# Gated linear attention with an MLP on one core: transposes of seven pairs by transfers within SBUF, DMA issues on two queues, a new order

## The chip, the cores and the metric

The kernel runs on one core of a Trainium2 chip. The metric is the device time of one execution in microseconds. Engines are named as in the profile: PE (TensorE, products), PEld (its weight loads), DVE (VectorE), ACT (ScalarE), POOL (GpSimd) and SP (SyncE, which here only issues transfers). A name with a q, as ACTq, is the engine's queue issuing a transfer.

## What is computed

Two parts in a row. The first is a recurrent linear attention with a decay for each key channel, over 4 batches, 8 heads, 768 steps and 48 channels:

```python
for t in range(S):
    state = alpha[:, :, t, :, None] * state + einsum('bhd,bhe->bhde', k[:, :, t], v[:, :, t])
    y[:, :, t] = einsum('bhd,bhde->bhe', q[:, :, t], state)
```

Its result, with the heads side by side, is a matrix x of 3072 x 384. The second part is an MLP with a cosine gate:

```python
h = x @ w_in            # 384 x 2048
g = h * cos(h)
out = g @ w_out         # 2048 x 384
```

## The kernel before

The sequence of one batch is cut into three pieces of 256 steps, so there are 12 pieces, called pairs (J = 0 to 11; J // 3 is the batch). A pair lies with two neighbouring steps on each of 128 partitions (e = 0, 1), and is worked as two chunks of 64 partitions (c = 0, 1).

The steps of one pair, by the names in the plan:

- `load a|k|q|v` (L108 to L119): one transfer of 384 KB each from SP's queue into rings of buffers (four for a, three for the others). `load a 3` waits for the last product of `yT 1`, so that later inputs stay behind the weights; everything behind it on SP's queue waits too. `w1`, `w2` (L131, L134): the weights, from POOL's queue.
- `mula`, `ln`, `cums0`, `cums`, `sub`, `icp`, `exps`, `eb`: the logarithm of the decay, its running sums by a triangular product on PE, and their exponentials on ACT (`eb` is four exponentials and the next pair's `ln` together). ACT loads a table whenever it changes between these and the cosine (L143, L388).
- `sk`, `sq` (L228, L232): k times the inverse decay into `kh`, q times the decay into `qh`, for e = 0 and 1, on DVE (":D" in the plan) or POOL. `kh` and `qh` are bf16 tiles of [128, e, head, 64], 48 channels padded to 64, three of each.
- `castv` (L235): v to bf16. `vst` (L241): four transfers of 64 KB within SBUF that stack the values of the two steps under each other in `vs` (two buffers), for pairs 3 to 11; for pairs 0 to 2, `vpe` and `vev` do it by products and evictions.
- `trans` (L274): 32 products on PE that transpose 64 x 128 pieces of `kh` and `qh` into PSUM. `evT` (L287): two copies of it into `qkT` in SBUF (three buffers), one for each chunk, on DVE or ACT (":A").
- `scores` (L295), `mask` (L300): 8 products for each chunk into `A_ps`, and the causal mask on DVE into `A_sb`.
- `outer`, `add`, `state` (L312, L326 or L328, L334), `decay`: the state at the chunk's end.
- `yT` (L361), `evy` (L372): the output y, transposed, from state and scores, and its eviction into `xT` on ACT or DVE.
- `m1` (L382), `sin` (L388), `gate` (L393), four of each: 12 products into `h_ps`, the cosine on ACT, the gate on DVE.
- `m2` (L411; L405 for the last), four quarters of four products for each half of the rows, `evo` (L423, L419) and `out` (L429): the output, its eviction into one of four buffers and its store of 192 KB on SP's queue; the last one goes in two halves, on ACT's and SP's queues.
- `idle` (L437): products of zeros that fill PE's time at the start.

The order is written out by hand: a table `PLAN` gives each step of each pair a place, all steps are sorted by place, and `tc.manual_schedule()` issues each engine's instructions in that order. Each engine and each queue works in order; waits between them come from the data. So a place says what stands ahead of a step on its own queue, not when it starts. An entry "2850:A" is place 2850 on ACT.

`h_ps`, `A_ps`, `T_ps` and some others share three turns of a PSUM tile of two banks (tag "h").

## Time and profile before

| | |
|---|---|
| median of 3 runs | 183.17 us (183.09 to 183.19) |
| profiled execution, its own time | 182.95 us |
| span of its profile | 181.1 us |
| mean granted TensorE clock | 0.999 |
| instructions | 5764 |
| read from HBM, written | 25.17 MB, 4.72 MB |
| tables loaded by ACT | 16, 1283 ns each |
| idle products on PE | 11.1 us busy |

The profile is of one execution. Its page gives the busy time of each engine, the chain of work that ended last (followed back from the last instruction, at each step to what released it), groups of instructions by source line with mean duration and the idle time before them, and the transfers by issue. The span goes from the first to the last instruction; the execution's own time has 1.85 us around it. In rows of the timeline, the columns are start, length, engine, line, operation, tiles; in brackets stands the idle time before and what ended it.

### The profile page before, as it was taken

The numbers are of one execution on the slowest core, as the hardware profiler recorded it, in microseconds if no ns is written. First come the engines' busy times: TensorE is split into PE (matmuls) and PEld (weight loads), VectorE is DVE, ScalarE is ACT, GpSimd is POOL, SyncE is SP. The second block draws the span as 40 slices with busy tenths as digits, with TensorE's granted clock in tenths as the row PEclk, the third lists the DMA queues.
The fourth block names the chain that finished last, engine by engine and source line by source line (L and its number), as shares of the span: only waits on it lengthen the run. The fifth ranks groups of instructions, "written<-read, shape, count | busy, mean of one in ns | idle before, by whom it ended". The sixth has DMA issues, their size and how long they took to land.

```text
span 181.1 us, 5764 instructions
## 1 busy us (share of the span) xinstructions
PE 174.6 (96%) x2467; PEld 133.1 (73%) x2470; DVE 132.6 (73%) x181; ACT 128.5 (71%) x169; POOL 72.6 (40%) x104
## 2 busy tenths in 40 slices
PE   7999899988999999999999999999999999999993
PEld 2445689756697876876799759678787878879672
DVE  7189677668899898796869965896987886653700
ACT  3847677997888999898598995997457428544520
POOL 5046730369682625805895196297003010000000
PEclk9999999999999999999999999999999999999999
DMA  6999999999969978984939953662202400102022
GB/s 149 261 270 227 204 211 224 272 254 268 274 160 270 282 183 233 295 249 106 264 73 290 251 149 101 161 164 78 71 0 49 145 5 0 47 0 79 11 87 87
DMA packets 57801, 29.47 MB, mean 163 GB/s; under 512 B 50992, under 2 KB 56496, under 8 KB 57776
## 3 DMA queue, kind: packets, MB, share of 16 engines
q1 hardware_dynamic: 56256, 25.86, 57.3%
q0 software_dynamic: 1376, 3.15, 9.4%
q8 instruction: 19, 0.31, 0.7%
q10 hardware_dynamic: 144, 0.10, 0.2%
q14 instruction: 6, 0.05, 0.1%
HBM read 25.17 MB, written 4.72 MB: 165 GB/s over the span
## 4 chain that ended last, share of the span: by engine, by line
PE 89%; DMA 3%; ACT 2%; DVE 2%; POOL 1%; issue 1%; POOLq 0%
PE h_ps L382 34%; PE o_ps L411 30%; PE idle_ps L437 6%; PE y_ps L361 5%; PE A_ps L295 3%; DMA k<-in_k_dram 3%; PE T_ps L274 3%; PE U_ps L312 3%; PE o_last L405 1%; PE cums_h L162 1%; DVE gsb L393 1%; ACT c_sb L388 1%; PE cums L162 1%; POOL kh L228 1%; PE vs_ps L250 1%; ACT xT L372 1%
## 5 line engine op out<-in xcount | busy, mean ns | idle before, releaser
L393 DVE TENSOR_TENSOR gsb<-h_ps,c_sb 128x1024 bf16<-128x1024 f32 x48 | 57.9, 1221 | 22.2 <-ACT c_sb L388 21.6
L388 ACT ACTIVATE c_sb<-h_ps,halfpi 128x1024 bf16<-128x1024 f32 x48 | 53.2, 1115 | 27.0 <-PE h_ps L382 24.3
L382 PE MATMUL h_ps<-xT,w 128*128 128x256 bf16 x576 | 67.5, 273 | 0.3 <-DVE gsb L393 0.2
L411 PE MATMUL o_ps<-w,gsb 128*128 128x384 bf16 x368 | 66.2, 326 | 0.6 <-DVE o_sb L423 0.6
L382 PEld LDWEIGHTS <-w 128*128 128x128 bf16 x576 | 62.2, 114 | 3.2 <-issue 0.4
L411 PEld LDWEIGHTS <-gsb 128*128 128x128 bf16 x368 | 34.5, 98 | 21.3 <-issue 0.9
L334 POOL TENSOR_TENSOR un<-us,c 128x384 bf16<-128x384 f32 x20 | 16.9, 845 | 38.6 <-DVE us L326 35.9
L300 DVE TENSOR_TENSOR A_sb<-A_ps,msk 128x1024 bf16<-128x1024 f32 x24 | 28.8, 1215 | 2.6 <-PE A_ps L295 2.6
L232 POOL TENSOR_TENSOR qh<-q,cp 128x384 bf16<-128x384 f32 x13 | 13.4, 1031 | 14.7 <-ACT cp L216 12.4
L228 POOL TENSOR_TENSOR kh<-k,icp 128x384 bf16<-128x384 f32 x15 | 15.7, 1052 | 5.6 <-DMA k<-in_k_dram 5.4
L156 POOL TENSOR_TENSOR a<-a 128x384 f32<-128x384 f32 x9 | 9.0, 1002 | 13.1 <-DMA a<-in_alpha_dram 13.1
L437 PE MATMUL idle_ps<-zeros 128*128 128x512 bf16 x38 | 11.1, 438 | 1.4 <-DVE halfpi L77 1.2
L148 ACT ACTIVATE lna<-a 128x768 bf16<-128x768 f32 x12 | 10.1, 842 | 3.0 <-DMA a<-in_alpha_dram 3.0
L235 POOL CAST vp<-v 128x768 bf16<-128x768 f32 x12 | 10.5, 880 | 2.5 <-DMA v<-in_v_dram 2.5
L423 ACT COPY o_sb<-o_ps 128x384 f32<-128x384 f32 x13 | 6.1, 481 | 7.5 <-PE o_ps L411 7.4
L372 ACT CAST xT<-y_ps 128x384 bf16<-128x384 f32 x16 | 8.8, 599 | 2.9 <-PE y_ps L361 2.6
L143 ACT ACT_TABLE_LOAD x8 | 10.3, 1283 | 0.9 <-PEq L552 0.7
L287 ACT COPY qkT<-T_ps 128x1024 bf16<-128x1024 bf16 x10 | 9.8, 1016 | 1.0 <-PE T_ps L274 1.0
L388 ACT ACT_TABLE_LOAD x8 | 10.3, 1283 | 0.1
L287 DVE COPY qkT<-T_ps 128x1024 bf16<-128x1024 bf16 x14 | 9.2, 684 | 1.4 <-PE T_ps L274 1.4
L232 DVE TENSOR_TENSOR qh<-q,cp 128x384 bf16<-128x384 f32 x11 | 6.8, 627 | 4.5 <-ACT cp L216 2.9
L326 DVE TENSOR_TENSOR us<-U_ps,un 128x384 f32<-128x384 f32 x16 | 8.8, 550 | 1.4 <-PE U_ps L312 1.3
(70 smaller groups left out, 157.2 us busy)
## 6 DMA issues: line engine op xcount, KB each, us to landing
a<-in_alpha_dram SPq DMA_DIRECT2D x12, 384.0 KB, 6.1
q<-in_q_dram SPq DMA_DIRECT2D x12, 384.0 KB, 5.8
k<-in_k_dram SPq DMA_DIRECT2D x12, 384.0 KB, 5.7
v<-in_v_dram SPq DMA_DIRECT2D x12, 384.0 KB, 5.7
out_dram<-o_sb SPq DMA_DIRECT2D x23, 192.0 KB, 2.5
vs<-vp SPq DMA_DIRECT2D x36, 64.0 KB, 2.6
w<-in_moe_w_in_dram POOLq DMA_DIRECT2D x2, 768.0 KB, 9.4
w<-in_moe_w_out_dram POOLq DMA_DIRECT2D x4, 384.0 KB, 9.0
```

Of the source, the lines that this page charges most:

```text
L228: eng.tensor_tensor(out=kh_t[J % NQ][:, e, :, 0:D], in0=kqv["k", J][:, :, e], in1=icp_, op=ALU.mult)
L232: eng.tensor_tensor(out=qh_t[J % NQ][:, e, :, 0:D], in0=kqv["q", J][:, :, e], in1=cp, op=ALU.mult)
L235: nc.gpsimd.tensor_copy(out=vp_t[J % NV][:, :, :, 0:D].rearrange("s e h d -> s h e d"), in_=kqv.pop(("v", J)))
L287: apart(("T", J), copy(out=qkT_sb[J][:, c], in_=T_ps[J][:, c].rearrange("r n e s -> r n (e s)")))
L300: nc.vector.tensor_tensor(out=A_sb[J][:, c].rearrange("s a p t -> s (a p) t"), in0=A_ps.pop((J, c)).rearrange("s a p t -> s (a p) t"), in1 ...
L334: nc.gpsimd.tensor_tensor(out=u, in0=U_sum.pop(n), in1=c2_sb[J][:, :, c].unsqueeze(3).to_broadcast([C, NP, 2, D]), op=ALU.mult)
L372: apart(("y", J), copy(out=xT[J][:, :, c * C : (c + 1) * C].rearrange("r i (t e) -> r i e t", e=2), in_=y_ps[J][c][:, 0 : KT * C].rearrang ...
L382: nc.tensor.matmul(h_ps[J, u][:, f, :], cols, xT[J][:, kk, :], start=(kk == 0), stop=(kk == KT - 1))
L388: nc.scalar.activation(out=c_sb[J, u], in_=h_ps[J, u], func=AF.Sin, bias=halfpi, scale=1.0)
L393: nc.vector.tensor_tensor(out=gsb[J][:, u * FW : (u + 1) * FW], in0=h_ps.pop((J, u)), in1=c_sb.pop((J, u)), op=ALU.mult)
L411: nc.tensor.matmul(o_ps[J, c][:, 0:DM], gsb[J][:, ft, c * C : (c + 1) * C], w2[:, ft], start=(ft == 0), stop=(ft == NF - 1))
L437: nc.tensor.matmul(idle_ps[0], zeros[:, 0:C], zeros, start=True, stop=True)
```

## The change

`kh` and `qh` are laid out anew, [128, p, e, a, 64], where p is the pair of heads and a the head in it, so that 128 values of one p and e lie side by side. The products of `sk` and `sq`, `trans` and `outer` address the new layout; their sizes stay.

For pairs 5 to 11 `trans` and `evT` go. In their place stand `trd 1` (k) and `trd 0` (q): each issues two transfers from SP's queue, one for each chunk, that read 64 partitions of 1024 bf16 values in SBUF and write them transposed into `qkT`.

15 of the 24 stores, and the stacked copies (`vst`) of pairs 4 and 9, are issued from ACT's queue. `load` can name a queue too, and stays on SP. ACT's table of exponentials is asked for at the start of the schedule.

The table of places is new throughout. Some steps change engine: `sk` on DVE 9 to 4, `sq` on DVE 11 to 4 (the rest on POOL), `evy` on ACT 16 to 11, `evT` on ACT 10 to 3 and on DVE 14 to 7. The number of idle products goes from 41 to 40.

```diff
-            t = consts.tile([C, 2, H, 64], BF, tag=f"{nm}{r}", name=f"{nm}{r}")
+            shape = [C, NP, 2, 2, 64] if nm in ("kh", "qh") else [C, 2, H, 64]
+            t = consts.tile(shape, BF, tag=f"{nm}{r}", name=f"{nm}{r}")
...
     def scale_k(J, e, eng):
-        icp_ = icp_sb.pop((J, e)).rearrange("p (h d) -> p h d", h=H)
-        eng.tensor_tensor(out=kh_t[J % NQ][:, e, :, 0:D], in0=kqv["k", J][:, :, e], in1=icp_, op=ALU.mult)
+        icp_ = icp_sb.pop((J, e)).rearrange("s (p a d) -> s p a d", p=NP, a=2)
+        eng.tensor_tensor(out=kh_t[J % NQ][:, :, e, :, 0:D], in0=kqv["k", J][:, :, e].rearrange("s (p a) d -> s p a d", a=2),
+                          in1=icp_, op=ALU.mult)
...
-    def stack_v(J):
+    def stack_v(J, queue):
...
-                nc.sync.dma_start(out=vs[HC * e : HC * e + HC, c].rearrange("s h d -> s (h d)"),
-                                  in_=vp[HC * c : HC * c + HC, e].rearrange("s h d -> s (h d)"))
+                queue.dma_start(out=vs[HC * e : HC * e + HC, c].rearrange("s h d -> s (h d)"),
+                                in_=vp[HC * c : HC * c + HC, e].rearrange("s h d -> s (h d)"))
...
+    def trans_dma(J, i):
+        if J not in qkT_sb:
+            qkT_sb[J] = turn(sb, [C, 2, 2 * NP, C], BF, "qkT", "qkT", BUF["qkT"])
+        x = (qh_t, kh_t)[i][J % NQ]
+        for c in range(2):
+            r = slice(HC * c, HC * c + HC)
+            nc.sync.dma_start_transpose(
+                out=qkT_sb[J][:, c, i * NP : (i + 1) * NP].rearrange("r p (e s) -> r (p e) s", e=2),
+                in_=x[r].rearrange("s p e a d -> s (p e a d)"))
...
-            o_sb[J, c] = [(t, slice(0, DM), nc.sync)]
-
-    def store(J, c):
+            o_sb[J, c] = [(t, slice(0, DM), None)]
+
+    def store(J, c, queue):
...
-            eng.dma_start(out=rows[:, cols], in_=t)
+            (eng or queue).dma_start(out=rows[:, cols], in_=t)
...
-        "load a": "10 30 60 980 1020 1410 1750 2500 2520 2230 3070 3970",
-        "load k": "50 170 1170 1280 1540 2210 1970 3040 3440 3490 4690 5040",
-        "load q": "40 240 1040 1330 1840 2110 2370 3090 3750 4170 5220 4610",
-        "load v": "100 270 1220 1460 1950 2340 2940 2830 3940 3150 4250 4660",
+        "load a": "30 50 90 1170 1180 1590 1910 1650 3100 2930 3510 3500",
+        "load k": "10 310 1030 1300 1680 1380 2460 3200 3660 3930 4760 4960",
+        "load q": "200 290 1130 1310 1600 2060 2970 2990 2640 4120 4850 5070",
+        "load v": "120 490 1190 1470 2010 2220 2480 2710 4160 4220 4640 5360",
...
-        "sk 0": "250:D 510:D 1450:D 1500:D 2060 2320 2790:D 3630 4230 4320 4840 5510",
-        "sk 1": "260:D 440:D 1430 1510 1920 2460:D 3190 3670 4050 4640 4910:D 5340",
-        "sq 0": "190:D 540:D 1370:D 1640 1980 2360:D 2980:D 3710 4120 4380 5230:D 5210",
-        "sq 1": "220 570:D 1380 1550:D 2200 2480:D 3160:D 3450 3870 4440 5540 5300:D",
+        "sk 0": "250:D 520:D 1340:D 1510 2080 2600 3050 3570 4010 4810 4870 5490",
+        "sk 1": "270:D 570 1430 1660 2100 2430 3020 3870 3970 4780 4950 5190",
+        "sq 0": "420 320:D 1270 1690 2170 2530 3130 3580 3690 4440 5440 5230",
+        "sq 1": "230:D 380:D 1220:D 1710 2070 2770 3110 3620 3750 4720 4930 5270",
...
-        "vst": "- - - 1960 2820 3410 3430 3760 4970 5080 5550 5800",
+        "vst": "- - - 1830 2620:A 3070 3450 4080 4530 4880:A 5740 5930",
...
-        "trans": "280 610 1520 1730 2250 2770 3320 3800 4750 4770 5570 5560",
-        "evT 0": "330 650:A 1580:A 1870:A 2400 2850:A 3400 3890 4820:A 4860:A 5630 5700:A",
-        "evT 1": "300 690 1530 1800 2310 2900:A 3340:A 3900 4870 4780 5690:A 5650",
-        "scores 0": "470 710 1710 1940 2740 2910 3570 4180 4960 5310 5730 5920",
-        "scores 1": "340 730 1660 1900 2390 3360 3580 4330 4980 5320 5720 5710",
+        "trans": "470 680 1500 1770 2270 - - - - - - -",
+        "trd 1": "- - - - - 2820 3140 4110 4510 4830 5170 5640",
+        "trd 0": "- - - - - 2830 3170 3890 4360 4820 5530 5730",
+        "evT 0": "610 690:A 1670 1840:A 2360 - - - - - - -",
+        "evT 1": "480 720 1560 1800:A 2370 - - - - - - -",
+        "scores 0": "620 710 1730 1980 2570 2880 3540 4170 4730 5090 5630 5970",
+        "scores 1": "590 750 1580 1870 2580 3440 3550 4180 4740 5280 5620 5900",
...
-        "yT": "680 950 1890 2240 2890 3700 3770 4390 5110 5500 5960 6110",
+        "yT": "700 920:X 1850 2240 2860 3710 3680 4420 4970 5400 5890 6100",
...
-        "out 0": "2490 3030 3220 4150 4620 4800 5590 5850 6200 6420 6600 6700",
-        "out 1": "2540 3140 3330 3530 4810 5170 5480 5930 5980 6510 6660 6730",
+        "out 0": "2210:A 2730:A 3560 3480:A 4380 5320 5040 6320:A 6040:A 6620 6400 6640:A",
+        "out 1": "2410:A 2720:A 3470:A 3770:A 4600:A 4840 5700:A 5580:A 6130:A 6460 6540:A 6660",
...
-    IDLE = [(20, 9), (120, 2), (160, 14), (310, 1), (370, 4), (550, 5), (640, 5), (840, 1)]
+    IDLE = [(20, 14), (80, 6), (100, 2), (330, 5), (360, 1), (510, 10), (670, 2)]
...
     with tc.manual_schedule():
+        act_set("exp")
```

In the new order these steps of PE stand between the last scaled operand of a pair and its first `scores`: pair 5 (2770 to 2880) two quarters of `m2` and one `yT`; pair 6 (3130 to 3540) seven quarters, two `cums`, two `outer`, one `scores`; pair 7 (3870 to 4170) three `m1`, three quarters, one `cums`; pair 9 (4810 to 5090) four quarters, one `m1`, one `yT`, one `outer`, one `cums`; pair 10 (5440 to 5620) four quarters and one `m1`.

More of the change, by code (lines that the diff above doesn't have):

```diff
@@ L106, with load @@
     src = {"a": alpha, "k": k, "q": q, "v": v}
-    def load(nm, J):
+    def load(nm, J, queue):
         b, g = J // NJB, J % NJB
         t = turn(sb, [C, H, 2, D], FP, nm, nm, BUF["a" if nm == "a" else "in"])
-        dma = nc.sync.dma_start(
+        dma = queue.dma_start(
             out=t.rearrange("p h e d -> p h (e d)"),
@@ L439 @@
     copies = {"DVE": nc.vector.tensor_copy, "ACT": nc.scalar.copy}
+    queues = {"SP": nc.sync, "ACT": nc.scalar}
     mults = {"DVE": nc.vector, "POOL": nc.gpsimd}
     steps = {
-        "load": lambda J, nm: load(nm, J), "w1": load_w1, "w2": load_w2,
+        "load": lambda J, nm, queue="SP": load(nm, J, queues[queue]), "w1": load_w1, "w2": load_w2,
         "mula": mul_a, "ln": ln, "cums0": cums0, "cums": lambda J, other="": cums(J, "o" if other else "x"), "sub": sub, "icp": icp, "exps": exps, "eb": session,
         "sk": lambda J, e, eng="POOL": scale_k(J, e, mults[eng]), "sq": lambda J, e, eng="POOL": scale_q(J, e, mults[eng]),
-        "castv": cast_v, "vst": stack_v, "vpe": lambda J, c, other="": stack_v_pe(J, c, "o" if other else "x"),
-        "vev": lambda J, c, eng="DVE": evict_vs(J, c, copies[eng]), "decay": decay, "trans": trans,
+        "castv": cast_v, "vst": lambda J, queue="SP": stack_v(J, queues[queue]), "vpe": lambda J, c, other="": stack_v_pe(J, c, "o" if other else "x"),
+        "vev": lambda J, c, eng="DVE": evict_vs(J, c, copies[eng]), "decay": decay, "trans": trans, "trd": trans_dma,
         "evT": lambda J, c, eng="DVE": evict_T(J, c, copies[eng]), "scores": scores, "mask": mask, "outer": outer,
@@ L449 @@
         "m1": mlp1, "sin": cosine, "gate": gate, "m2": lambda J, c, part, other="": mlp2(J, c, part, "x" if other else "o"), "evo": lambda J, c, eng="ACT": evict_o(J, c, copies[eng]),
-        "out": store, "idle": idle,
+        "out": lambda J, c, queue="SP": store(J, c, queues[queue]), "idle": idle,
     }
     PLAN = {
[66 rows of a table removed]
[68 rows of a table added]
     }
-    IDLE = [(20, 9), (120, 2), (160, 14), (310, 1), (370, 4), (550, 5), (640, 5), (840, 1)]
+    IDLE = [(20, 14), (80, 6), (100, 2), (330, 5), (360, 1), (510, 10), (670, 2)]
     order = []
```

12 lines of the change are left out of this document (7 added, 5 removed), and 98 rows, old and new, of the table PLAN.

## Prediction

> **What bounds the kernel now.** I read the page first: the span, the busy shares and the shares of the chain of waits.
>
> ```profile
> span 181.1 us, 5764 instructions
> PE 174.6 (96%) x2467; PEld 133.1 (73%) x2470; DVE 132.6 (73%) x181; ACT 128.5 (71%) x169; POOL 72.6 (40%) x104
> ...
> PE 89%; DMA 3%; ACT 2%; DVE 2%; POOL 1%; issue 1%; POOLq 0%
> ```
>
> TensorE (PE) is busy for 96% and carries 89% of the chain. An average hides stages, so the next view was the busy time of each engine by stretch (columns: length, then busy us and instructions of PE, PEld, DVE, ACT, POOL, then granted clock, DMA share, GB/s).
>
> ```profile
> 0.00:21.34 21.34, 19.30 (x254) 9.97 (x258) 14.12 (x42) 12.53 (x23) 10.53 (x29) 1.00 1.07 222
> 21.34:175.40 154.06, 152.72 (x2184) 120.72 (x2184) 118.11 (x139) 115.22 (x145) 62.12 (x75) 1.00 0.64 158
> 178.03:181.10 3.07, 0.00 (x0) 0.00 (x0) 0.36 (x1) 0.01 (x1) 0.00 (x0) 0.94 0.19 64
> ```
> ```profile
> 40.00:50.00 10.00, 9.48 (x215) 6.52 (x213) 8.43 (x12) 8.46 (x17) 7.27 (x9) 1.00 1.18 272
> 50.00:60.00 10.00, 10.00 (x161) 8.16 (x154) 9.85 (x13) 8.71 (x11) 5.68 (x7) 1.00 0.98 219
> 60.00:70.00 10.00, 10.00 (x130) 8.33 (x129) 9.33 (x13) 9.63 (x13) 3.24 (x6) 1.00 0.85 205
> ```
>
> Three stretches, then. Up to 21.34 us, where the first product of the MLP starts, the input loads set the pace and PE is filled up with idle products. To about 50 us the DMA engines are still full (share 1.18) and PE has small gaps. From 50 us on PE is busy for all of every 10 us, at the full clock, so there a piece of PE work that goes away comes off the end one for one, as long as nothing else becomes late. The last 3 us, the eviction and store of the final half, stay.
>
> **What is removed.** Pairs 5 to 11 lose `trans`, 32 transposing products each. Their price is their share of PE's time in order of the chain (start, length, what), not the 190 ns of one, since they are pipelined.
>
> ```profile
> 69.16 0.47 PE T_ps L274 x32
> ...
> 91.06 0.57 PE T_ps L274 x32
> ...
> 136.82 0.93 PE T_ps L274 x64
> ...
> 144.62 1.30 PE o_ps L411 x8
> ...
> 146.59 0.90 PE y_ps L361 x56
> ...
> 161.03 1.31 PE h_ps L382 x12
> ```
>
> These are pairs 5 and 7, then 10 and 11 together: 1.97 us for four pairs, 0.49 each, 3.4 for seven. The page gives the whole line 3% of the chain, 5.4 us for twelve pairs, so 3.2 for seven. I take **-3.3 us**. All of it lies after 65 us, where PE has no gaps. (The last three rows price what follows: a quarter of `m2`, four products, 0.65 us; `yT` 0.90; a step of `m1` 1.31.)
>
> With the transposes go 14 evictions of `qkT`, and work is dealt out anew between the other engines.
>
> ```profile
> L287 ACT COPY qkT<-T_ps 128x1024 bf16<-128x1024 bf16 x10 | 9.8, 1016 | 1.0 <-PE T_ps L274 1.0
> L287 DVE COPY qkT<-T_ps 128x1024 bf16<-128x1024 bf16 x14 | 9.2, 684 | 1.4 <-PE T_ps L274 1.4
> L228 POOL TENSOR_TENSOR kh<-k,icp 128x384 bf16<-128x384 f32 x15 | 15.7, 1052 | 5.6 <-DMA k<-in_k_dram 5.4
> L232 POOL TENSOR_TENSOR qh<-q,cp 128x384 bf16<-128x384 f32 x13 | 13.4, 1031 | 14.7 <-ACT cp L216 12.4
> L232 DVE TENSOR_TENSOR qh<-q,cp 128x384 bf16<-128x384 f32 x11 | 6.8, 627 | 4.5 <-ACT cp L216 2.9
> ...
> L372 ACT CAST xT<-y_ps 128x384 bf16<-128x384 f32 x16 | 8.8, 599 | 2.9 <-PE y_ps L361 2.6
> L300 DVE TENSOR_TENSOR A_sb<-A_ps,msk 128x1024 bf16<-128x1024 f32 x24 | 28.8, 1215 | 2.6 <-PE A_ps L295 2.6
> L326 DVE TENSOR_TENSOR us<-U_ps,un 128x384 f32<-128x384 f32 x16 | 8.8, 550 | 1.4 <-PE U_ps L312 1.3
> ```
>
> Counting the plan's entries: ScalarE evicts 3 instead of 10 (-7.1 us), VectorE 7 instead of 14 (-4.8). Five products of k and seven of q move from VectorE to GpSimd: about 12 x 0.63 = -7.6 on VectorE, 5 x 1.05 + 7 x 1.03 = +12.5 on GpSimd, which goes from 72.6 to 85 us, below half of the span. I put that at nothing for GpSimd as an engine; its cover is its idle time, 108 us. If that cover fails it shows as late operands of the transfers, and is priced there. The new layout of `kh` and `qh` keeps the element counts of every instruction: nothing, with the 1052 and 1031 ns of two differently strided products as bounds of 2%. Loading ScalarE's table at the start costs nothing, as that load is already ScalarE's first instruction.
>
> **What is added.** Each of the seven pairs gets four transposing transfers of 64 x 1024 values, 128 KB, on SP's queue: 28. The trace has none. The nearest rows, by queue time and by landing:
>
> ```profile
> 7.15 1.45 SPq L111 DMA_DIRECT2D k<-in_k_dram  x1
> ...
> 58.54 1.91 SPq L429 DMA_DIRECT2D out_dram<-o_sb  x1
> ...
> 64.19 3.53 SPq L241 DMA_DIRECT2D vs<-vp  x4
> ...
> 101.36 0.38 SPq L111 DMA_DIRECT2D v<-in_v_dram  x1
> ...
> 123.84 0.33 SPq L429 DMA_DIRECT2D out_dram<-o_sb  x1
> 124.28 2.38 SPq L241 DMA_DIRECT2D vs<-vp  x4
> ```
> ```profile
> k<-in_k_dram SPq DMA_DIRECT2D x12, 384.0 KB, 5.7
> ...
> vs<-vp SPq DMA_DIRECT2D x36, 64.0 KB, 2.6
> ```
>
> The copies of stacked values are also SBUF to SBUF: 0.60 to 0.88 us of queue each, 2.6 to landing. A load is the upper row: up to 1.45 of queue, 5.7 to landing. A transfer of twice a copy's bytes lies between and nearer the copy: I take 1.2 us of queue and 3 us to landing. Below nothing is excluded, since each one is a wait that did not exist.
>
> [...]
>
> Whether PE waits for a landing depends on the work written between the last scaled operand and the first `scores` of the pair. Adding up PE's steps in the new order: 2.2 us for pair 5 (two quarters of `m2`, one `yT`), 5.8, 6.1, 16.6, 5.4, 3.9 and 11.9 for pairs 6 to 11. Into that must go the product (1.03), one landing (3.0), and in pair 10, whose second chunk comes first, one more queue slot (1.2). Only two pairs are short: pair 5 by 1.8, pair 10 by 1.3. But GpSimd is often ahead of its place in the order:
>
> ```profile
> 83.42 1.00 POOL L232 TENSOR_TENSOR qh<-q,cp 128x384 bf16<-128x384 f32 x1 [6.93 <-ACT cp L216]
> ```
>
> There it stood 6.9 us for its operand. So the two shortages are an upper case; a fifth of 3.1 is **+0.6 us**. What is late next is `mask`, then `yT` of the same pair, all behind `scores` on PE's in-order queue.
>
> ScalarE's queue gets 15 stores and 8 copies. At 0.33 to 1.91 a store and 0.60 to 0.88 a copy this is 10 to 36 us; its own queue carries little else, so the unloaded rows are nearer: about 0.5 and 0.65, 12.7. Against it stand the -7.1 and five `evy` that go to VectorE (about 0.6 each, -3): ScalarE's total rises by about 2.6 us. All but the last two of these stores wait for an eviction written at least 130 places earlier, so their own waits hardly block ScalarE (the last stands 30 places behind VectorE's eviction, in the tail, before ScalarE's final copy); behind it stand the `sin` steps, which `gate` and then `m2` need. The narrow place is 60 to 70 us, 9.63 busy of 10: a copy of pair 4 and six stores come there or soon after. I take **+0.3 us**.
>
> **What is moved in the first two stretches.**
>
> ```profile
> 4.36 0.84 ACT L148 ACTIVATE lna<-a 128x768 bf16<-128x768 f32 x1 [2.33 <-DMA a<-in_alpha_dram]
> ...
> 5.87 0.84 ACT L148 ACTIVATE lna<-a 128x768 bf16<-128x768 f32 x1 [0.67 <-DMA a<-in_alpha_dram]
> ...
> 8.96 1.57 DVE L228 TENSOR_TENSOR kh<-k,icp 128x384 bf16<-128x384 f32 x2 [0.94 <-ACT icp L208]
> ...
> 10.60 0.41 PE L274 MATMUL T_ps<-ident_bf,kh 64*128 64x64 bf16 x16
> ...
> 11.93 0.82 POOL L235 CAST vp<-v 128x768 bf16<-128x768 f32 x1 [2.28 <-DMA v<-in_v_dram]
> ```
>
> Loads land 1.5 us apart (first, second and sixth load at 4.36, 5.87 and 11.93). The first a becomes the second load, and the first q the sixth: it lands near 11.9, so the first product of q, two of k (1.57) and one more of q on GpSimd (1.0) put the transposes of pair 0 near 15 us instead of 10.60. Before, 16 idle products and waits lay between there and the MLP; after, about 5.6 us of VectorE work lies there (three evictions at 0.68, two masks at 1.2, two adds at 0.55), then `yT` and two `evy`: first MLP product at 21.0 to 23.0 us, against 21.34. I take **+0.7 us** (-0.3 to +1.7). In return k and q of pair 2 no longer stand behind the gate on `yT` of pair 1, and the waits list shows what that could save, with the other gap of that stretch:
>
> ```profile
> PE o_ps L411 <- DVE o_sb L423: 0.6, 1, 0.6
> PE U_ps L312 <- POOL vp L235: 0.4, 1, 0.4
> ```
>
> At most 1.0 us; as the weights now share the DMA engines with these two loads, I take **-0.5 us**.
>
> **The sum.** The profiled execution took 182.95 us, 181.1 of span and 1.85 around it: 182.95 - 3.3 + 0.6 + 0.3 + 0.7 - 0.5 = 180.75. The median of the runs, 183.17, is 0.2 higher; on its footing **181.0 us**. Its own range, with the unknowns at their better and worse ends short of the rivals, is 179.0 to 182.6.
>
> **The rivals.**
>
> ScalarE becomes the bound. If its queue slots cost 2 us more than taken in the full stretch, `sin` is late, and PE with it, since nothing there is spare: 181.0 + 2.0 = 183.0. For: 9.63 of 10. Against: the removed evictions and moved `evy` free 10 us in the whole.
>
> Landings come late (the slower side). At 4.15 us, the middle of the two rows, and with GpSimd at its written place, pair 5 waits 3.0 and pair 10 waits 2.5: 5.5 in place of 0.6, 185.9. It decides from a landing of about 2.9 us on: without any wait the change gains 2.8, and the two waits are (landing - 1.2) + (landing - 1.7). For: SP's queue is in order and loads stand ahead of the transfers. Against: GpSimd's idle time.
>
> SP's queue cannot carry the transfers. Between the transposes of pair 5 (69.16) and of pairs 10 and 11 (136.82) lie 68 us; 18 loads at about 1, four pairs of copies at 2.4 and five stores take about 31, which leaves 37 for 28 transfers, 1.3 each. At a load's 1.45 this costs 28 x 0.15 = 4 us, 185; at the 2.38 of four copies 28 x 1.1 = 30 us, 211. [...]
>
> The start slips further: +2.3 instead of +0.7 as q lands behind the weights too, 182.6.
>
> **Chances.** Forecast 0.50, ScalarE 0.15, late landings 0.22, SP's queue 0.08, the start 0.05. What a measurement here can tell from no change is 0.2%, 0.37 us. ScalarE's case is split evenly over the three signs, the start's 0.03 to 0.02, and the rest of the rivals lies above. Faster: 0.50 + 0.05 + 0.03 = 0.58; within: 0.05 + 0.02 = 0.07; slower: 0.05 + 0.22 + 0.08 = 0.35. The range 179.0 to 187.5 leaves out the top of the late landings, most of SP's queue and a little below: about 0.15.
>
> **What would show it.** Right: 5 pairs of `T_ps` on the page instead of 12, PE busy 10.00 in every stretch from 50 us on, transposing transfers landing in about 3 us, the first `h_ps` between 21 and 23 us. Wrong: idle time before `A_ps` ended by a DMA (late landings), SP's transfers back to back with `scores` behind them (queue), idle time before `m2` or `gate` ended by ScalarE, a first `h_ps` past 23 us.

## The result and the profile after

| | before | after |
|---|---|---|
| median of 4 runs each | 183.13 us (182.99 to 183.19) | 191.08 us (189.76 to 193.82) |
| ratio, 95% interval | | 1.041 [1.036, 1.046] |
| profiled execution, its own time | 182.95 us | 189.76 us |
| span of its profile | 181.1 us | 188.0 us |
| mean granted TensorE clock | 0.999 | 0.982 |
| instructions | 5764 | 5316 |

The change makes the kernel 4.1% slower; 181.0 us was forecast, and 191.1 lies outside the range. (Ratios leave disturbed runs out, so one can stand a little below the ratio of its two medians.)

The page of the changed kernel: span, busy shares, shares of the chain of waits.

```profile
span 188.0 us, 5316 instructions
PE 173.5 (92%) x2245; PEld 130.4 (69%) x2245; DVE 125.0 (66%) x167; ACT 119.1 (63%) x157; POOL 82.9 (44%) x116
...
PE 56%; DMA 12%; SPq 10%; ACT 7%; POOL 6%; DVE 4%; issue 2%; ACTq 0%; POOLq 0%; DVEq 0%
```

PE has less work than before, and its share of the chain falls from 89% to 56%: over two fifths of it lie elsewhere now. Busy time by stretch (columns as in the prediction) shows where.

```profile
0.00:22.66 22.66, 19.21 (x257) 9.83 (x258) 13.90 (x41) 11.88 (x23) 11.32 (x29) 1.00 1.07 240
...
40.00:50.00 10.00, 10.00 (x218) 6.68 (x211) 6.92 (x10) 8.68 (x17) 7.68 (x10) 1.00 1.05 271
...
120.00:130.00 10.00, 5.71 (x106) 4.02 (x105) 2.51 (x3) 2.19 (x3) 1.94 (x2) 0.91 0.88 213
130.00:140.00 10.00, 8.65 (x66) 6.27 (x66) 6.90 (x9) 8.12 (x11) 7.21 (x8) 0.75 0.34 75
```

The start is 1.3 us longer (22.66 against 21.34), the gaps of 40 to 50 us are closed, and a hole that was not there before lies at 125 to 131 us, with a lower clock behind it. Until 128.9 us PE, VectorE and ScalarE all rest in it. The chain of waits through the hole (start, length, what):

```profile
120.59 0.53 SPq L443
...
122.45 5.82 DMA out_dram<-o_sb
...
128.35 0.47 ACTq L245
...
128.92 1.12 ACT c_sb L402
...
130.07 1.24 DVE gsb L407
...
131.34 0.61 PE A_ps L309 x8
```

Read from below: PE's `scores` wait for the gate, which frees their PSUM turn; the gate waits for the cosine `c_sb`; the cosine stands on ScalarE behind a transfer that ScalarE issues (L245, the last of four copies of pair 9's stacked values); and that issue waited for a store on the *other* queue, SP's, to land. ScalarE's own timeline gives the length of it.

```profile
120.12 1.11 ACT L402 ACTIVATE c_sb<-h_ps,halfpi 128x1024 bf16<-128x1024 f32 x1 [0.61 <-PE h_ps L396]
120.86 7.96 ACTq L245 DMA_DIRECT2D vs<-vp  x4
128.92 1.11 ACT L402 ACTIVATE c_sb<-h_ps,halfpi 128x1024 bf16<-128x1024 f32 x1 [7.68 <-DMA out_dram<-o_sb]
```

Four issues that I had priced at 0.65 us each, and that took 0.47 to 0.61, held ScalarE for 7.96 us from the first to the end of the last, which was issued only at 128.35. No data ties those copies to that store: it writes the output of pair 6. So not every wait in this kernel comes from the data. What ties them stands in the trace's semaphore records. There the 137 transfers of SP's and ScalarE's queues report their landings to eight counters, 17 or 18 transfers to each, in one turn over both queues. On the six counters for which every landing is recorded there are 97 transfers that follow another on the same counter, and none of them was issued before the earlier one had landed. Around the hole (issue, queue, transfer, its counter, counters that the queue waited for ahead of the issue, landing):

```
122.45 SP   store of pair 6           108   105 (ScalarE's eviction)      128.27
120.86 ACT  copy 1 of pair 9's values 118   118, 103, 99 (POOL's cast)    123.20
121.97 ACT  copy 2                    101   101                           126.63
122.47 ACT  copy 3                    104   106                           127.17
128.35 ACT  copy 4                    108   108, 107                      130.66
```

Copy 4 is the next transfer after the store on counter 108, so in the turn the eighth after it, and it was issued 0.08 us after the store had landed; copies 1 and 2 went out 0.10 and 0.02 us after the landings ahead of them on their counters. (Copy 3 has no wait for its own, since ScalarE had awaited counter 104 at an eviction at 118.97.) The store took 5.82 us to land, where the stores of this run took 1.8 to 5.9 us and 3.4 in the median; why it was among the slowest was not looked into. In the kernel before, where all but one half store stood on SP's queue, the 101 transfers that follow another on their counter were issued 0.58 us or more after its landing, so none of them shows such a hold. On ScalarE it held the next cosine: 7.68 us of idle time stand before it in the row above. The hole costs more than itself (steps of 2 us, columns as above; the clock is the third number from the end):

```profile
128.00:130.00 2.00, 0.00 (x0) 0.00 (x0) 0.00 (x0) 1.08 (x2) 0.00 (x0) 0.53 0.64 116
130.00:132.00 2.00, 0.66 (x9) 0.46 (x9) 1.93 (x3) 1.97 (x4) 0.00 (x0) 0.50 0.79 171
132.00:134.00 2.00, 2.00 (x7) 0.90 (x7) 1.48 (x4) 1.98 (x5) 1.64 (x3) 0.50 0.81 188
134.00:136.00 2.00, 2.00 (x15) 1.57 (x13) 0.93 (x1) 0.82 (x1) 2.00 (x3) 0.76 0.02 6
```

From 128.1 to 135.0 us the granted clock is half (the means of 0.53 and 0.76 are of the steps in which this begins and ends), and PE works in it from 131.34 on: eight products of `m2` take 2.74 us (at 131.89), where at 1.00 they took 1.46 (at 119.92). By the steps, 0.66 x 0.5 + 2.00 x 0.5 + 2.00 x 0.24 = 1.8 us of PE's work lost. PE's other new idle times and the hole itself, from its timeline (in brackets the idle time before and what ended it):

```profile
72.05 0.40 PE L309 MATMUL A_ps<-qkT 48*128 48x128 bf16 x8 [0.71 <-DMA qkT<-qh]
...
117.49 0.40 PE L309 MATMUL A_ps<-qkT 48*128 48x128 bf16 x8 [0.23 <-DVE gsb L407]
118.62 1.47 PE L396 MATMUL h_ps<-xT,w 128*128 128x256 bf16 x12 [0.73 <-DVE gsb L407]
...
131.34 0.61 PE L309 MATMUL A_ps<-qkT 48*128 48x128 bf16 x8 [5.64 <-DVE gsb L407]
```

The account: start 1.3, hole 5.6, clock 1.8, other waits 1.7, and 0.3 for a longer last stretch behind PE's end; less the two gaps that closed (1.0) and 2.9 for the transposes. The 2.9 is read from the two pages: PE is busy for 173.5 us against 174.6, which is 1.1 less, and 2.9 less without the 1.8 of the clock. The sum is 6.8 us, and the two profiled executions differ by 6.8.

### The profile page after: what moved, and what is told of

Same layout as the page of the kernel before. It is cut to its first block, busy times and chain, and to the rows that moved or that the text cites. A ratio compares the mean times of both kernels' runs of the same rounds, so it can differ in the third digit from the quotient of the medians.

```text
span 188.0 us, 5316 instructions
## 1 busy us (share of the span) xinstructions
PE 173.5 (92%) x2245; PEld 130.4 (69%) x2245; DVE 125.0 (66%) x167; ACT 119.1 (63%) x157; POOL 82.9 (44%) x116
## 4 chain that ended last, share of the span: by engine, by line
PE 56%; DMA 12%; SPq 10%; ACT 7%; POOL 6%; DVE 4%; issue 2%; ACTq 0%; POOLq 0%; DVEq 0%
PE h_ps L396 24%; PE o_ps L425 22%; SPq L299 5%; SPq L113 4%; DMA a<-in_alpha_dram 3%; DMA out_dram<-o_sb 3%; PE y_ps L375 3%; DMA v<-in_v_dram 3%; DMA qkT<-qh 3%; POOL qh L235 2%; PE A_ps L309 2%; DVE gsb L407 2%; DVE A_sb L314 2%; POOL kh L230 2%; PE o_last L419 1%
## 5 line engine op out<-in xcount | busy, mean ns | idle before, releaser
L425 PE MATMUL o_ps<-w,gsb 128*128 128x384 bf16 x368 | 68.3, 331 | 0.0
L235 POOL TENSOR_TENSOR qh<-q,cp 128x384 bf16<-128x384 f32 x20 | 20.2, 1019 | 8.4 <-DMA q<-in_q_dram 8.4
L230 POOL TENSOR_TENSOR kh<-k,icp 128x384 bf16<-128x384 f32 x20 | 19.9, 1002 | 8.1 <-PE A_ps L309 3.7
L309 PE MATMUL A_ps<-qkT 48*128 48x128 bf16 x192 | 9.2, 221 | 6.9 <-DVE gsb L407 5.9
L309 PEld LDWEIGHTS <-qkT 48*128 48x128 bf16 x192 | 5.8, 95 | 11.0 <-issue 8.6
L239 POOL CAST vp<-v 128x768 bf16<-128x768 f32 x12 | 9.9, 822 | 8.0 <-DMA v<-in_v_dram 8.0
L437 DVE COPY o_sb<-o_ps 128x384 f32<-128x384 f32 x10 | 5.6, 555 | 11.0 <-PE o_ps L425 7.5
L386 DVE CAST xT<-y_ps 128x384 bf16<-128x384 f32 x13 | 7.2, 584 | 2.9 <-PE y_ps L375 2.9
```

Source lines behind the costliest of these rows:

```text
L230: eng.tensor_tensor(out=kh_t[J % NQ][:, :, e, :, 0:D], in0=kqv["k", J][:, :, e].rearrange("s (p a) d -> s p a d", a=2), in1=icp_, op=ALU.mult)
L235: eng.tensor_tensor(out=qh_t[J % NQ][:, :, e, :, 0:D], in0=kqv["q", J][:, :, e].rearrange("s (p a) d -> s p a d", a=2), in1=cp, op=ALU.mult)
L309: nc.tensor.matmul(A_ps[J, c][:, a, p, :], qkT[r, c, NP + p, :], qkT[r, c, p, :], start=True, stop=True)
L425: nc.tensor.matmul(o_ps[J, c][:, 0:DM], gsb[J][:, ft, c * C : (c + 1) * C], w2[:, ft], start=(ft == 0), stop=(ft == NF - 1))
L437: copy(out=t, in_=o_ps.pop((J, c))[:, 0:DM])
```

## The experiments

Two theories stood against each other at first: the eight counters shared by both queues (the loss is that one wait), and a general cost of the new order or of transfers that come late. Fifteen kernels were run; the kernel before beside them had medians of 183.09 to 183.21 us.

**The copies of pair 9 back on SP.** The changed kernel with one letter of its table taken out.

```diff
-        "vst": "- - - 1830 2620:A 3070 3450 4080 4530 4880:A 5740 5930",
+        "vst": "- - - 1830 2620:A 3070 3450 4080 4530 4880 5740 5930",
```

> The changed kernel with one entry edited: the stacked copies of pair 9 go back to SP's queue. Theory (ScalarE stands in the issue of the fourth copy until a store on SP's queue has landed, since the eight completion counters are handed out in turn over both queues): the 7.7 us wait of ScalarE, the 5.6 us gap of PE at 126 us and the lower clock after it all go, about 7.5 us of the span of 188.0, so about 182.3 us. Rival (the transposing transfers and the traffic around them are what is late): the gap stays in some form near 126 us, at most 2 us are won, 187 us or more.

Measured: 184.46 us (183.79 to 185.92), ratio 1.008 [1.005, 1.011]. One letter gives back 6.6 of the 8 us; the hole is gone and the clock is 1.0 as long as PE works. The theory's number was still 2 us too good. The stretch behind its start, and PE's waits in it, show why:

```profile
22.72:178.00 155.28, 151.47 (x1980) 119.14 (x1980) 110.75 (x126) 106.80 (x134) 71.57 (x87) 1.00 0.78 176
```
```profile
71.95 0.40 PE L309 MATMUL A_ps<-qkT 48*128 48x128 bf16 x8 [0.52 <-DMA qkT<-qh]
...
90.08 0.55 PE L375 MATMUL y_ps<-A_sb,vs 128*32 128x128 bf16 x25 [0.79 <-DMA vs<-vp]
...
118.93 1.47 PE L396 MATMUL h_ps<-xT,w 128*128 128x256 bf16 x12 [0.73 <-DVE gsb L407]
...
143.98 1.47 PE L396 MATMUL h_ps<-xT,w 128*128 128x256 bf16 x12 [1.51 <-DVE gsb L407]
```

Behind the start PE is idle for 155.28 - 151.47 = 3.8 us, where the kernel before had 154.06 - 152.72 = 1.3 in as long a stretch. So even without the hole the relief of the transposes does not arrive.

**The store of pair 6 earlier.** If the counter is what binds, the copies may stay on ScalarE when the transfer eight places ahead of the last one is another, earlier one. Edit: the store of pair 6's first half goes from place 5040 to 4845.

```diff
-        "out 0": "2210:A 2730:A 3560 3480:A 4380 5320 5040 6320:A 6040:A 6620 6400 6640:A",
+        "out 0": "2210:A 2730:A 3560 3480:A 4380 5320 4845 6320:A 6040:A 6620 6400 6640:A",
```

> The changed kernel with one entry edited: the store of pair 6, first half, on SP's queue stands at place 4845 instead of 5040. The copies of pair 9 stay on ScalarE's queue, but the fourth now waits for the counter of the store issued ahead (1.9 us earlier in the changed kernel's trace). Theory: the wait of ScalarE gets shorter by 2 to 4 us and PE's gap with it, 185 to 188 us. Rival (issuing a copy from ScalarE is slow while transposing transfers are in flight): the wait stays at 7 to 8 us, 191 us.

Measured: 185.26 us (184.01 to 186.17), ratio 1.011 [1.008, 1.014]. The four issues, still on ScalarE, take 3.38 us instead of 7.96, and PE's longest wait in that region is 0.81. ScalarE issues the same copies as before this edit; what has changed is that this store goes out earlier on SP, and with it which transfers stand eight places ahead; which of them copy 4 followed here is not shown. With the list above, that speaks for the counter, and against a cost of issuing on ScalarE as such.

**All stores and copies on SP, the transfers kept.** The two copies lose their ":A" too.

```diff
-        "out 0": "2210:A 2730:A 3560 3480:A 4380 5320 5040 6320:A 6040:A 6620 6400 6640:A",
+        "out 0": "2210 2730 3560 3480 4380 5320 5040 6320 6040 6620 6400 6640",
...
-        "out 1": "2410:A 2720:A 3470:A 3770:A 4600:A 4840 5700:A 5580:A 6130:A 6460 6540:A 6660",
+        "out 1": "2410 2720 3470 3770 4600 4840 5700 5580 6130 6460 6540 6660",
```

> All 15 stores and both pairs' copies back on SP's queue, transposing transfers and order kept. Theory: ScalarE is never held by a transfer, but SP has 23 more issues of 0.4 to 0.7 us in front of and between its transposing transfers: no gap at 126 us of the kind seen, small new waits of scores on transfers, 182 to 185 us. Rival (SP's queue is the narrow place and needed the relief): 186 us or more, with PE waiting for qkT in several pairs.

Measured: 187.24 us, but over a spread from 184.18 to 188.29; ratio 1.012 [1.007, 1.018]. The profiled execution, 184.18, waits 1.65 and 1.05 us for the gate and the state's addition, and has no hole. It says only that the new order is slower than the kernel before in this arrangement too; where the spread comes from was not found.

**The kernel before in the new layout.** The code of the changed kernel with the table of the kernel before: new layout of `kh` and `qh` and the early table load, all else as before.

> The changed code with the old table of places: new layout of kh and qh, early table load, no transposing transfer, no store on ScalarE's queue. If the layout costs nothing: 183.1 us, the kernel before. If the strided products or the products that read the new layout are slower: more, and the means of kh and qh on DVE and POOL show it.

Measured: 183.25 us, ratio 1.004 [1.000, 1.007]. The layout costs nothing that matters, so this code is the ground for the next runs, each with one part of the change.

**The queue alone.** The order of the kernel before; the same 15 stores and eight copies from ScalarE, all transposes on PE.

```diff
-        "vst": "- - - 1960 2820 3410 3430 3760 4970 5080 5550 5800",
+        "vst": "- - - 1960 2820:A 3410 3430 3760 4970 5080:A 5550 5800",
...
-        "out 0": "2490 3030 3220 4150 4620 4800 5590 5850 6200 6420 6600 6700",
+        "out 0": "2490:A 3030:A 3220 4150:A 4620 4800 5590 5850:A 6200:A 6420 6600 6700:A",
...
-        "out 1": "2540 3140 3330 3530 4810 5170 5480 5930 5980 6510 6660 6730",
+        "out 1": "2540:A 3140:A 3330:A 3530:A 4810:A 5170 5480:A 5930:A 5980:A 6510 6660:A 6730",
```

> The order of the kernel before with another part of the change alone: the same 15 stores and the copies of stacked values of pairs 4 and 9 are issued by ScalarE, at the places where the kernel before has them; all transposes stay on TensorE. Theory (issuing costs ScalarE its 0.4 to 0.65 us per transfer, and a transfer also waits until the eighth before it over both queues has landed; ScalarE then holds its cosines back): 183.5 to 187 us, with ScalarE issues held for over 1 us somewhere and gates of VectorE waiting for c_sb. Rival (the hold in the changed kernel needs the transposing transfers, and without them ScalarE's queue is free of cost): 182.9 to 183.4 us, no ScalarE issue over 1 us.

Measured: 189.44 us (187.09 to 190.57), ratio 1.028 [1.022, 1.035]. This part alone, without one transposing transfer, costs 6.2 us in the old order. It does not do so in the way that the theory said, though; no issue is held for over 1 us at the places where PE waits:

```profile
67.75 2.76 PE L425 MATMUL o_ps<-w,gsb 128*128 128x384 bf16 x16 [1.59 <-ACT o_sb L437]
...
76.70 0.87 PE L375 MATMUL y_ps<-A_sb,vs 128*32 128x128 bf16 x32 [2.40 <-DMA vs<-vp]
```
```profile
61.85 0.39 ACTq L443 DMA_DIRECT2D out_dram<-o_sb  x1
...
67.22 0.48 ACT L437 COPY o_sb<-o_ps 128x384 f32<-128x384 f32 x1 [2.84 <-DMA out_dram<-o_sb]
...
71.68 0.51 ACTq L245 DMA_DIRECT2D vs<-vp  x1
```

Here ScalarE's in-order stream makes the transfers late. It comes to two stores only from 61.85 on, so at 64.4 its own next eviction finds no `o_sb` buffer and waits 2.84 us for a landing; and it comes to pair 4's copies at 71.68, where SP had issued them from 64.19 on (the row in the prediction), and the values' products wait 2.40 for them.

**Stores alone and copies alone.** To part the two, the same edit with only its `out` rows and with only its `vst` row.

> The order of the kernel before with only the 15 stores issued by ScalarE, the copies of pairs 4 and 9 again by SP. Theory A (the stores carry the loss of 189.4 us: they are issued only when ScalarE comes to them, so the o_sb buffers come back late to its own evictions): 186.5 to 190 us, and ScalarE still waits some 3 us for o_sb near 64 us. Theory B (the copies carry it, as in the changed kernel): 183.1 to 184 us.

> The order of the kernel before with only the copies of stacked values of pairs 4 and 9 issued by ScalarE, all stores by SP. Theory A (the stores carry the loss): 183.1 to 184 us. Theory B (the copies carry it: they are held until transfers of SP's queue have landed, or come late to the values' products): 185 to 189 us, with TensorE waiting for vs or for gates.

Measured: 184.59 us with the stores, ratio 1.008 [1.006, 1.010]; 188.27 us with the copies, ratio 1.029 [1.026, 1.033]. Theory B holds in the main (the stores came out 0.6 us above its range): eight copies cost 5.1 us, fifteen stores 1.4, about the sum of the run with both. Where the stores' 1.4 us lies stayed open; PE's waits from 50 to 178 us come to 0.4 us in that run. In the copies' run PE waits once, and pays again by the clock:

```profile
75.67 1.14 PE L375 MATMUL y_ps<-A_sb,vs 128*32 128x128 bf16 x32 [2.94 <-DMA vs<-vp]
```
```profile
74.00:76.00 2.00, 0.33 (x13) 0.27 (x17) 0.00 (x0) 0.36 (x1) 1.99 (x4) 0.81 0.64 134
76.00:78.00 2.00, 2.00 (x39) 1.27 (x33) 1.14 (x3) 1.12 (x2) 0.83 (x1) 0.50 1.04 253
```

In the changed kernel, where the copies of pair 4 stand at an earlier place, no wait of PE is put down to them, and those of pair 9 cost the hole. So the price of a transfer on ScalarE is a matter of its place and of what is in flight, not of its 0.5 us.

**Three pairs' transposes alone.** The order of the kernel before, with transposing transfers behind the operands of pairs 7, 8 and 9 and nothing on ScalarE. (`evT 1` loses the same entries; the load of q of pair 10 moves from place 5220 to 5035, ahead of the transfers.)

```diff
-        "trans": "280 610 1520 1730 2250 2770 3320 3800 4750 4770 5570 5560",
+        "trans": "280 610 1520 1730 2250 2770 3320 - - - 5570 5560",
...
-        "evT 0": "330 650:A 1580:A 1870:A 2400 2850:A 3400 3890 4820:A 4860:A 5630 5700:A",
+        "evT 0": "330 650:A 1580:A 1870:A 2400 2850:A 3400 - - - 5630 5700:A",
...
+        "trd 1": "- - - - - - - 3755 4255 5043 - -",
...
+        "trd 0": "- - - - - - - 3756 4256 5042 - -",
```

> As the run with six pairs, but transposing transfers for pairs 7, 8 and 9 alone. Theory: half of the gain, 1.4 us less 0.1 to 0.3, so 181.7 to 182.1 us. Rival (relief given back): 182.8 to 183.5 us, no better than the kernel before, and the run with six pairs no better than this one.

Measured: 183.40 us, ratio 1.002 [0.999, 1.005]: the rival. PE works 1.4 us less behind the first 20 us and is not done earlier. The reason stands in PE's timeline, first of the kernel before and then of this run, at the two places that the transposes left (pair 7, then pairs 8 and 9):

```profile
90.99 0.41 PE L274 MATMUL T_ps<-ident_bf,kh 64*128 64x64 bf16 x16
91.24 0.40 PE L274 MATMUL T_ps<-ident_bf,qh 64*128 64x64 bf16 x16
...
91.84 8.04 PE L382 MATMUL h_ps<-xT,w 128*128 128x256 bf16 x72
...
115.50 0.43 PE L312 MATMUL U_ps<-vp,kh 64*128 64x96 bf16 x6
...
117.22 0.82 PE L411 MATMUL o_ps<-w,gsb 128*128 128x384 bf16 x4
```
```profile
92.11 8.11 PE L396 MATMUL h_ps<-xT,w 128*128 128x256 bf16 x72 [0.36 <-DVE xT L386]
...
115.84 0.85 PE L326 MATMUL U_ps<-vp,kh 64*128 64x96 bf16 x24
...
117.54 0.81 PE L425 MATMUL o_ps<-w,gsb 128*128 128x384 bf16 x4 [0.84 <-DVE o_sb L437]
```

Between `yT` and `m1` PE has to wait for the eviction `xT` anyway, and between `outer` and `m2` for an `o_sb`. The kernel before had put the transposes there. PE then shows as busy for all of the 10 us, and yet the transposes were not what it was busy for the sake of: they filled waits, which opened as soon as they left (0.36 + 0.84 of 1.4 us).

**The waits filled.** The same, with other work in those two places: the last output product of pair 4 behind `yT 6`, and on VectorE the eviction ahead of the state's addition.

```diff
-        "m2 1 3": "1400 1830 2720 3210 3680 4430 5000 5430 5740 6320 6570 6710",
+        "m2 1 3": "1400 1830 2720 3210 3805 4430 5000 5430 5740 6320 6570 6710",
...
-        "evo 0": "1270:D 1630 2590 3120 3540 4470:D 4740:D 5470 6120:D 6400:D 6560 6670",
+        "evo 0": "1270:D 1630 2590 3120 3540 4470:D 4725:D 5470 6120:D 6400:D 6560 6670",
```

> The run with three transferred pairs (183.40 us) with two steps moved: the eviction of pair 6's first output stands ahead of the state's addition of pair 8 on VectorE, and the last output product of pair 4 behind the values of pair 6, where the transposes of pair 7 stood. Theory (the transposes had filled waits of TensorE, 0.36 us for xT and 0.84 us for o_sb, which opened once they left; with other work in those two places the relief comes through): 181.9 to 182.6 us, and the two idle times gone. Rival (the time is bound by something else, VectorE's and ScalarE's chain or the SP queue): 183.2 to 183.6 us, the idle times come up elsewhere.

And as the control, the two moved steps with all transposes on PE:

> The order of the kernel before with all transposes on TensorE and only the two moves of the filling run: pair 6's first output evicted ahead of the state's addition of pair 8, the last output product of pair 4 behind the values of pair 6. Theory (the moves fill waits that only opened when the transposes left): 183.1 to 183.5 us, no gain. Rival (the moves gain by themselves and the transfers of three pairs give nothing): 182.7 to 183.0 us.

Measured: 182.91 us, ratio 0.998 [0.995, 1.000], between the theory's range and the rival's, and 183.31 us for the moves alone, ratio 1.001 [1.000, 1.002]. The moves gain nothing where the transposes still fill the waits, and 0.4 to 0.5 us where they have left. Both idle times are gone; a new one of 0.54 us (before the `cums` of pair 11, waiting for ScalarE) took part of the relief.

**A fourth pair, and more places filled.** Pair 10's transposes go too (`trans` and both `evT` lose its entry), and then two sets of moves on top of that, each apart from the other:

```diff
-        "trd 1": "- - - - - - - 3755 4255 5043 - -",
+        "trd 1": "- - - - - - - 3755 4255 5043 5475 -",
...
-        "trd 0": "- - - - - - - 3756 4256 5042 - -",
+        "trd 0": "- - - - - - - 3756 4256 5042 5545 -",
```

> As the run with the two moved steps, and pair 10's transposes by transfers too. Theory: 0.2 to 0.5 us below that run, 181.5 to 182.3 us, if the last of the four transfers lands ahead of the scores (operands at 130 us, four transfers of 1.3 us on the queue and 3 us to land are 138, the scores come at 140). Rival (the transfers come late behind the copies of pairs 8 and 9 on SP): TensorE waits before the scores for the transfer, 182.5 to 184 us.

```diff
-        "cums": "90 290 460 1350 1760 2140 2510 3050 3520 3810 4560 4880",
+        "cums": "90 290 460 1350 1760 2140 2510 3050 3520 3810 4560 4945",
...
-        "sub": "- - - 1420 1810 2270 2550 3240 3560 4030 4680 4900",
+        "sub": "- - - 1420 1810 2270 2550 3240 3560 4030 4680 4955",
...
-        "castv": "350 660 1560 1740 2530 3010 3370 3420 4700 4110 4600 5030",
+        "castv": "350 660 1505 1740 2530 3010 3370 3420 4700 4110 4600 5030",
```

> As the run with four transferred pairs (182.62 us), with two more places filled where TensorE still waits in it: the running sum of pair 11 goes behind the next output product (0.55 us before cums at 117.66 there), and on POOL the cast of pair 2's values goes ahead of the second key scaling of pair 3 (0.68 us before U_ps at 43.79 there). Theory (TensorE's time comes through wherever the wait behind it is filled): 0.8 to 1.2 us less, 181.4 to 181.9 us. Rival (the next wait in the chain takes it over): 182.4 to 182.8 us.

```diff
-        "castv": "350 660 1560 1740 2530 3010 3370 3420 4700 4110 4600 5030",
+        "castv": "350 660 1505 1740 2530 3010 3370 3420 4700 4110 4600 5030",
...
-        "state 0": "630 880 1850 2030 2800 3590 3690 4280 4830 4930 5620 6010",
+        "state 0": "630 880 1735 2030 2800 3590 3690 4280 4830 4930 5620 6010",
```

> The run with four transferred pairs (182.62 us) with the cast of pair 2's values ahead of the second key scaling of pair 3 on POOL, and the state's decay of pair 2 ahead of the cast of pair 3's values, which waited there for its load (0.97 us of TensorE in the run that filled two places). Theory: the 0.7 us before U_ps come through now, 181.7 to 182.2 us. Rival (the loads set this stretch, the next wait for one takes it): 182.5 to 183.2 us.

Measured: 182.62 us with pair 10 too, ratio 0.998 [0.994, 1.001]. The time lies in the rival's range, but the wait for transfers that the rival named does not appear. Then two more places: 183.37, ratio 1.001 [1.000, 1.002], a miss. The waits came up one step on, as the rival said:

```profile
49.23 0.46 PE L375 MATMUL y_ps<-qkT,un 128*32 128x128 bf16 x20 [0.97 <-POOL un L348]
...
122.94 0.81 PE L425 MATMUL o_ps<-w,gsb 128*128 128x384 bf16 x4 [0.69 <-ACT cp L218]
```

On POOL the state's decay `un` stood behind a cast that waited for its load; and the later `cums` made ScalarE's exponentials late. The third version leaves `cums` where it was and puts `un` ahead of that cast: 182.07 us (181.51 to 183.10), ratio 0.994 [0.991, 0.996]. This is faster than both kernels, by 0.6% against the kernel before: four pairs by transfers, four steps and a load moved, nothing but the last half store on ScalarE's queue. How much of it the last two moves would give without transfers was not tried.

**Six pairs' transposes alone.** Pairs 6 to 11 by transfers in the order of the kernel before (`trans` and `evT` lose those entries, the load of q of pair 10 moves as above). This kernel computes wrong values, and why was not found; its times and waits are used for the schedule alone.

```diff
+        "trd 1": "- - - - - - 3155 3755 4255 5043 5475 5512",
...
+        "trd 0": "- - - - - - 3215 3756 4256 5042 5545 5546",
```

> The plan of the kernel before (its order of all steps), with one part of the change alone: the TensorE transposes and their two evictions of pairs 6 to 11 give way to transposing transfers on SP, issued right behind the operands; all stores and copies of stacked values stay where the kernel before has them. Theory (the transposes are worth their TensorE time, and what the change lost lies in its order and in what ScalarE issues): 6 pairs by 0.47 us of TensorE work are 2.8 us, less 0.1 for the new layout and up to 0.5 for late landings and a busier SP queue: 180.2 to 181.0 us, five to seven T_ps groups gone. Rival (TensorE's relief is given back, because its stretches in this part wait for VectorE and ScalarE, or SP's queue is then too full): 182.5 to 184 us, with new idle time of TensorE after 80 us that ends with a DMA or with VectorE.

Measured: 190.75 us, ratio 1.041 [1.037, 1.046], 10 us above the theory. PE's timeline and the queue's:

```profile
118.61 0.81 PE L425 MATMUL o_ps<-w,gsb 128*128 128x384 bf16 x4 [1.76 <-DVE o_sb L437]
...
145.76 0.85 PE L309 MATMUL A_ps<-qkT 48*128 48x128 bf16 x24 [3.16 <-DMA qkT<-qh]
```
```profile
105.99 3.67 SPq L299 DMA_TRANSPOSE qkT<-kh  x2
109.70 3.27 SPq L299 DMA_TRANSPOSE qkT<-qh  x2
...
116.48 1.90 SPq L443 DMA_DIRECT2D out_dram<-o_sb  x2
118.48 2.40 SPq L245 DMA_DIRECT2D vs<-vp  x4
```

With stores, copies and loads all left on SP, its queue has hardly a gap from 93 to 148 us; the stores come late (DVE waits for `o_sb`), and the last transposes land after PE has come to the scores. Room on the queue is not the whole matter, though: the run with all stores and copies on SP has one pair more by transfers, and in its profiled execution PE waits for none of them. So the places of the transfers count too, and how much each counts was not parted.

**The new order with the transposes back on PE.** It was to measure what the transfers are worth in the new order.

```diff
-        "trans": "470 680 1500 1770 2270 - - - - - - -",
+        "trans": "470 680 1500 1770 2270 2871 3302 4152 4412 4911 5532 5831",
...
-        "evT 0": "610 690:A 1670 1840:A 2360 - - - - - - -",
+        "evT 0": "610 690:A 1670 1840:A 2360 2872:A 3303 4153 4413:A 4912:A 5534 5833:A",
```

> The changed kernel with the copies of pair 9 on SP (184.46 us) and in it the seven pairs' transposes put back on TensorE with their two evictions each, shared between VectorE and ScalarE; order of all other steps and the stores on ScalarE as in the changed kernel. What the transfers are worth in the new order. Theory (worth their TensorE time there too): 184.5 + 7 x 0.47 = 187.8 us, 187 to 189 with the evictions. Rival (the new order is bound by VectorE's and ScalarE's steps and not by TensorE): 184.5 to 186 us.

Measured: 205.63 us, ratio 1.120 [1.116, 1.125]. Far above both theories, so it tells neither. PE waited 2.61 us for a gate, 3.09 for the state's addition and 1.72 and 1.11 for evictions of `qkT`: the transposes take PSUM turns of their own (tag "h"), the places free for them are few, and where I put them they held up other steps. The worth of the transfers in the new order stays open.

## Why the prediction was wrong, step by step

- **The step that failed most is the price of ScalarE's queue.** The prediction wrote that the stores' "own waits hardly block ScalarE" and took +0.3 us for 15 stores and eight copies. It looked only at waits for data. Measured on the changed kernel, taking four of those copies off ScalarE gives 6.6 us; measured alone in the old order, stores and copies together cost 6.2. The two stores in the tail cost nothing, as was said: they held ScalarE for 3.68 us, but its last copy waited longer for PE. Two things showed in place of it: a transfer waited for the landing of the eighth before it, on the other queue, and held ScalarE meanwhile (the 7.96 us at the hole), and transfers were issued no earlier than ScalarE's stream came to them (PE's waits of 2.40 and 2.94 us in the old order). The rival "ScalarE becomes the bound" had the right engine, but put the place at 60 to 70 us and the price at 2 us.
- **The worth of the transposes was read too high.** The claim that in stretches with PE at 10.00 a piece that goes away comes off "one for one, as long as nothing else becomes late" fell: of three pairs' 1.4 us none came through, and some 0.4 once two other steps stood in their places. The rider "as long as" was the whole matter. The -3.3 us was PE's work (2.9 by the two pages), not the kernel's time.
- **The transfers were sized rightly in the middle.** 1.2 us of queue and 3 to landing were taken. The fastest pairs of issues took 2.52 us (1.26 each), others up to 4.36; landings took 2.6 to 7.0 us, 3.0 in the median, but those of q were slower:

```profile
qkT<-kh SPq DMA_TRANSPOSE x14, 2.8
qkT<-qh SPq DMA_TRANSPOSE x14, 4.2
```
- **Late landings** cost about what was taken, +0.6 against 0.71 us at pair 5, but by two errors that offset each other. The transfer that PE waited for there took about 5 us to land (issued at 66.95, `scores` at 72.05), and q's median of 4.2 is close to the rival's 4.15, so the rival's landings did occur. Its waits did not, since GpSimd was further ahead than its place: pair 5's last operand was done at 65.41, 5.9 us before PE came to the `scores`, where its written place leaves 1.2. Pair 10 did not wait.
- **SP's queue** carried the 28 transfers in the change's arrangement. In the run with six pairs, in the old order and with all else on SP, PE waited 3.16 us for the last of them.
- **Start and gaps**: +0.7 was taken and 1.3 measured, inside its range; -0.5 was taken, and the gaps closed wholly, 1.0.
- The **sign** and the range failed with the first two steps. Of what was named as a sign of being wrong, "idle time before `m2` or `gate` ended by ScalarE" is what appeared: the gate of 130.07 waited for `c_sb`.

## What to carry to other kernels

Before a transfer moves to the queue of an engine that computes, ask what the issue itself can wait for: here the trace's semaphore records listed it, a completion counter shared with another queue included, and what stood behind it on that engine waited too (the cosine for 7.68 us). A PE that is busy for all of a stretch may be busy with fillers: before pricing work that leaves, look at what stands right behind it and whether its operand would be there earlier. When a piece of work leaves, put other work in its place in the order, and look one wait further, since the next one is often only a few tenths behind.

## What the runs showed of the hardware that was not expected

The granted clock fell to half around much shorter rests of PE than the hole's 5.64 us: it went to 0.50 after waits of 2.94 and 2.40 us (copies alone, queue alone), and of 1.76 in the run with six pairs, whose steps of 2 us read

```profile
118.00:120.00 2.00, 1.39 (x11) 0.83 (x11) 1.14 (x3) 0.09 (x1) 0.08 (x1) 0.84 1.17 312
120.00:122.00 2.00, 2.00 (x8) 0.81 (x6) 0.99 (x2) 1.53 (x4) 1.20 (x1) 0.50 0.77 234
122.00:124.00 2.00, 2.00 (x25) 1.32 (x24) 0.97 (x2) 1.45 (x2) 2.00 (x4) 0.81 0.82 201
```

while it stayed at 1.00 after 1.51 us (copies of pair 9 on SP, a mean of 1.00 from 22.72 to 178 us) and 1.65 us (all on SP, 1.00 from 90 to 100 us, in which PE is idle for those 1.65). The wait of 1.76 us cost twice, once by itself and once by the half clock behind it: the steps come to (0.16 + 0.50 + 0.19) x 2 = 1.7 us of full clock missing, which is 3.4 us at half.

The steps around the other two falls, 0.81, 0.50 and 0.84 with the copies alone and 0.80, 0.50 and 0.85 with the queue alone, come to 3.4 us at half as well, and those of the hole to 6.8. No run varied the length of a rest or its place alone, so what decides on a fall is not shown.
